# Two decode layers on one core: an added idle product ahead of the second layer's second queries, and w2's second and third pieces cut elsewhere

## The chip, the cores and the metric

One core of a Trainium2 chip runs the program. The metric is the device time of one execution in microseconds, the median of several runs. TensorE is PE in the profile, VectorE DVE, ScalarE ACT, GpSimd POOL; SyncE's queue, which issues nearly all transfers, is SP.

## The reference, cut to what matters

One token goes through four steps: attention, MLP, attention, MLP. Both attentions use the same weights and caches, and so do both MLPs.

```python
def _A_ref(x, k_cache, v_cache, wq, wo):            # 32 heads, 4096 keys, 128 a head, D = 512
    q = (x @ wq).reshape(B, Sq, H, Dh).transpose(0, 2, 1, 3)
    p = softmax(einsum("bhqd,bhkd->bhqk", q, k_cache) * (Dh ** -0.5))
    return einsum("bhqk,bhkd->bhqd", p, v_cache)... @ wo
def _B_ref(x, w1, b1, w2, b2):                      # F = 1376
    return gelu(x @ w1 + b1) @ w2 + b2
x = x + A(layernorm(x)); x = x + B(layernorm(x))
x = x + A(layernorm(x)); x = x + B(layernorm(x))
```

Everything is float32. The k and v caches are 64 MB each (eight groups of 8 MB), so that the caches, read twice but for what is kept on the chip, make nearly all of the traffic.

## The kernel before, in words

The 32 heads are worked in eight groups of four heads (G = 8). For a group, the 4096 keys are cut into eight blocks c of 512. `scores` (L201) makes four products a block, one a head, into the PSUM tile pS; `exponentials` (L206) takes the row maximum on DVE and the exponential on ACT (L214); `weights` (L217) turns the exponentials with four TensorE transposes into pO and copies them out on DVE (L222); `values` (L232) makes four products a block with the v cache into pO; `head` and `out_product` (L256, L276) normalize and multiply by wo. The queries of the next group are made by `query_block` (L189), sixteen small products into pO, and `queries` (L194), which turns pO on DVE (L150).

Nearly all of SBUF is one tile, `arena`, cut by hand: a ring of three homes of 8 MB (A_AT, B_AT, C_AT) for whole groups of k or v, and behind them places for weights (SHARED, SCRATCH, PAIR) that w1, w2, wo, wq and pieces of k use one after the other. All loads go out on SP's queue through `load` (L78), in program order. A load whose place is still being read, or was written by an earlier load, waits on SP for that; every load behind it waits as well. Products keep their program order on TensorE (`matmul`, L83). The order of DVE's and ACT's instructions is the program builder's: it may put a later line ahead of an earlier one. What waits for what follows from which bytes of the arena or of PSUM two instructions share.

**The change of layers.** The first layer ends with group 7. Its k lies in C_AT, its v in A_AT, and most of group 6's v is kept in B_AT, the rest in six PSUM banks pK. The second layer begins with group 7's k and v, which are still there, and goes on with group 6's v. In between stands the first MLP (`mlp`, L285). It multiplies x by four rows of w1 at SHARED; after row c's products it issues piece c of w2 into the same place, as W2_AT_CHANGE (L49) cuts it, and a fifth piece behind the first DVE step (L302). A piece is a range of w2's eleven blocks of 256 KB. Then come gelu and the eleven blocks of the second product (L310), eight passes on TensorE each. Behind blocks 3, 7 and 9, `behind_w2` (L435) issues the load of wq for the second layer's second queries (1 MB, SHARED, where blocks 0 to 3 lay) and the first six quarter blocks of group 6's k. Behind blocks 4, 7 and 10 stands `idle` (L165): a product with a zero operand and as streaming operand the first 512 or 256 columns at C_AT, whose result nothing uses.

**The second layer's start** (L450 to L485). First queries, then eight blocks of scores against group 7's k in C_AT. When block 0 is scored, `begin_k` (L430) loads four quarter blocks of group 6's k over it, at C_AT (L458); when block 1 is scored, four more; behind block 5 the rest (L460), then a pair of weights (L462). Then come `exponentials`, the second queries' `query_block` (L464), which reads wq at SHARED, `queries`, `weights`, and `values` against A_AT. ACT copies group 6's v out of the PSUM banks (L476): the first two copies go to SHARED and SHARED + U, where wq's first two blocks lie, once these are read. When A_AT's last block is used, SP issues group 5's k into it (8 MB). Scores and values of group 6 follow, and from there five more groups in the ring.

Of the kernel before, what the change touches and what calls it, by code (L numbers as in the profile page):

```python
# [25 lines left out]
FB = 11  # L26
W1C = FJ * J
EPS = 1e-5
U = 512
# [16 lines left out]
BY_PE = 3  # L46
W1_AT_END = ((0, 2), (2, 3), (3, 4))
LAST = ((0, 4), (4, 6), (6, 7), (7, 8))
W2_AT_CHANGE = ((0, 2), (2, 5), (5, 8), (8, 10), (10, 11))  # L49
W2_AT_END = ((0, 4), (4, 8), (8, 10), (10, 11))  # L50


# [1 line left out]
def decode_layers(ctx: ExitStack, tc: tile.TileContext, x, k, v, w, w1, b1, w2, b2, out):  # L54
# [10 lines left out]
    def small(name, n=1):  # L65
        if name not in places:
            a = sum(b - a for a, b in places.values())
            places[name] = a, a + n
        a, b = places[name]
        assert b <= 160 and b - a == n  # L70
        return smalls[:, a:b]
# [3 lines left out]
    def at(first, n):  # L75
        return arena[:, first : first + n]

    def load(first, src):  # L78
        t = at(first, src.shape[-1])
        tc.keep_in_program_order(nc.sync.dma_start(t, src))  # L80
        return t

    def matmul(*a, **kw):  # L83
        tc.keep_in_program_order(nc.tensor.matmul(*a, **kw))  # L84
# [7 lines left out]
    def of_w(row, i, n):  # L92
        return w[row][:, NC * i : NC * (i + n)]
# [24 lines left out]
    pS, pO = (psum.tile([P, 512], F32, name=n) for n in ("pS", "pO"))  # L118
# [9 lines left out]
    def of_32(t, n, i=0):  # L128
        return t[:, : 32 * n].rearrange("p (c q) -> p c q", q=32)[:, :, i]
# [9 lines left out]
    def pairs(t):  # L139
        return t[:, :8].rearrange("p (c i) -> p c i", i=2)  # L140

    def turned(src, wide=False):

        t = work.tile([P, P], F32, name="turned")
        if wide:
            for j in range(J):
                q = slice(32 * j, 32 * j + 32)
                nc.vector.transpose(t[q], src[q, P * j : P * (j + 1)])  # L148
        else:
            nc.vector.transpose(t, src[:, :P])  # L150
        return t

    def set_x(xin0, scale, xin1, queries=True):
        s = small("x_sum")
        t = x_wide if queries else small("x1", 8)
        if not queries:
            nc.gpsimd.memset(pairs(t)[:, :, 1], 1.0)
        x = pairs(t)[:, :, 0]
        nc.vector.scalar_tensor_tensor(x, xin0, scale, xin1, op0=ALU.mult, op1=ALU.add, accum_out=s)
        if queries:  # L160
            for j in range(1, J):
                nc.gpsimd.tensor_copy(pairs(t[:, 32 * j :])[:, :, 0], x)  # L162
        return t, s

    def idle(to, n=U):  # L165
        matmul(to[:, :n], zero[:, 0:1].to_broadcast([P, P]), at(C_AT, n), start=True, stop=True)
# [6 lines left out]
    def mean_of(xs, s):  # L173
        nm = minus_mean(s, pS[:, 0:1])
        xc, sq, ss, negm = small("xc", 4), small("sq", 4), small("ss"), small("negm")
        nc.vector.tensor_scalar(xc, pairs(xs)[:, :, 0], nm, None, op0=ALU.add)
        nc.vector.scalar_tensor_tensor(sq, xc, 1.0, xc, op0=ALU.mult, op1=ALU.mult, accum_out=ss)
        nc.vector.tensor_copy(negm, nm)
        return negm, ss

    def rstd_of(ss):
        nv = minus_mean(ss, pS[:, 1:2])
        ve, r = small("ve"), small("rstd")
        nc.vector.tensor_scalar(ve, nv, -1.0, EPS, op0=ALU.mult, op1=ALU.add)
        nc.vector.memset(pS[:, 0:2], 0.0)
        nc.gpsimd.tensor_tensor(r, ve, power, op=ALU.pow)
        return r

    def query_block(c, xs, wt):  # L189
        for j in range(J):  # L190
            matmul(pO[32 * j : 32 * j + 2, :P], pairs(xs)[:, c, :], wt[:, c, P * j : P * (j + 1)],
                   start=(c == 0), stop=(c == 3))
# [13 lines left out]
    def exponentials(sc, nsc):  # L206
        nc.vector.tensor_reduce(ml[:, 0:1], pS, axis=AX.X, op=ALU.max)  # L207
        mt, m, bias = work.tile([P, 32], F32, name="mt"), small("m"), work.tile([P, 32], F32, name="mt")
        nc.vector.transpose(mt, ml)
        nc.vector.tensor_reduce(m, mt[:, :C], axis=AX.X, op=ALU.max)  # L210
        nc.vector.tensor_scalar(mb[:, :C], m.to_broadcast([P, C]), nsc, None, op0=ALU.mult)
        nc.vector.transpose(bias, mb)  # L212
        p = at(SCRATCH, U)
        nc.scalar.activation(p, pS, AF.Exp, bias=bias[:, 0:1], scale=sc, accum_out=ml[:, 0:1])  # L214
        return p
# [69 lines left out]
    def mlp(xs, s, w1_t, w2_t, load_w2=None, behind_w2=None):  # L285
        xb = small("xb", 4)
        nc.gpsimd.tensor_tensor(xb, pairs(xs)[:, :, 0], b2c, op=ALU.add)
        for c in range(4):
            for j in range(J):
                matmul(pO[32 * j : 32 * j + 2, :FJ], pairs(xs)[:, c, :], w1_t[c][:, FJ * j : FJ * (j + 1)],  # L290
                       start=(c == 0), stop=(c == 3))
            if c == 0:
                nm, ss = mean_of(xs, s)
            if c == 1:
                r = rstd_of(ss)
            if load_w2:
                load_w2(c)
        idle(pS)
        ht = at(SCRATCH, 32 * FB)
        nc.vector.transpose(ht, pO[:, : 32 * FB])  # L300
        h, u, a, z, t, g = (small(f"gelu_{i}", FB) for i in "huaztg")
        nc.vector.scalar_tensor_tensor(h, of_32(ht, FB, 1), nm, of_32(ht, FB), op0=ALU.mult, op1=ALU.add)  # L302
        if load_w2:
            load_w2(4)
        nc.vector.scalar_tensor_tensor(u, h, r, b1c, op0=ALU.mult, op1=ALU.add)
        nc.vector.scalar_tensor_tensor(a, u, 0.044715, u, op0=ALU.mult, op1=ALU.mult)
        nc.vector.scalar_tensor_tensor(z, a, 1.0, u, op0=ALU.add, op1=ALU.mult)
        nc.scalar.activation(t, z, AF.Tanh, scale=float(np.sqrt(2.0 / np.pi)))
        nc.vector.scalar_tensor_tensor(g, t, 1.0, u, op0=ALU.add, op1=ALU.mult)  # L309
        for c in range(FB):  # L310
            for j in range(J):
                matmul(pS[32 * j : 32 * j + 1, :P], g[:, c : c + 1], w2_t[c][:, P * j : P * (j + 1)],
                       start=(c == 0), stop=(c == FB - 1))
            if load_w2:
                behind_w2(c)
                if c in (4, 7, FB - 1):
                    idle(pO, U if c == 4 else U // 2)
        return of_32(turned(pS), 4), xb

    def load_w1(first, a, b):  # L320
# [2 lines left out]
    def load_w2(first, a, b):  # L323
        load(first + U * a, w2[:, U * a : U * b])

    def in_rows(first, n, rows):
        return [at(first + n * i, n) for i in range(rows)]
# [107 lines left out]
    def behind_w2(c):  # L435
        if c == 3:
            load(SHARED, of_w((G - 1) % 2, G - 2, 1))
        if c == 7:
            begin_k(SHARED + NC, 4)
        if c == 9:  # L440
            begin_k(SHARED + 2 * NC, 2)

    own, xb = mlp(x1, s1, in_rows(SHARED, W1C, 4), in_rows(SHARED, U, FB),
                  lambda i: load_w2(SHARED, *W2_AT_CHANGE[i]), behind_w2)
    xs, s = set_x(own, 0.5, xb)
# [15 lines left out]
            k_t.append(at(KEPT_K, U))  # L461
    pair = load(C_AT + 24 * U, of_w(g % 2, g - 1, 2))  # L462
    p = exponentials(sc, nsc)
    for c in range(4):  # L464
        query_block(c, xs, wq_t)
    z = queries(pO, negm)
# [20 lines left out]
    for n in range(2, G):  # L487
# [18 lines left out]
        own = head_out(rl, wo_t, last=True)  # L506
    x1, s1 = set_x(own, 1.0, acc, queries=False)
    own, xb = mlp(x1, s1, in_rows(A_AT, W1C, 4), in_rows(A_AT + 11 * U, U, FB))
    y = small("y", 4)
    nc.vector.scalar_tensor_tensor(y, own, 0.5, xb, op0=ALU.mult, op1=ALU.add)  # L510
# [43 lines left out]
```

## Time and profile before

| | |
|---|---|
| median of 3 runs | 673.06 us (672.82 to 673.77) |
| the profiled execution's own time | 673.26 us |
| its span | 671.5 us |
| moved into SBUF | 285.88 MB, 426 GB/s over the span |
| PE / DVE / ACT / POOL busy | 59% / 49% / 3% / 1% of the span |

The profiled execution took 0.20 us more than the median. The span runs from the first to the last instruction; 1.8 us of the execution lie around it. A transfer's time to landing counts from its issue on SP, so that issue plus time is the moment it has landed. A product in float32 is two passes in the profile, so a count of products there is twice that of the code.

### The profile page before, as it was taken

The numbers are of one execution on the slowest core, as the hardware profiler recorded it, in microseconds if no ns is written. First come the engines' busy times: TensorE is split into PE (matmuls) and PEld (weight loads), VectorE is DVE, ScalarE is ACT, GpSimd is POOL, SyncE is SP. The second block draws the span as 40 slices with busy tenths as digits, with TensorE's granted clock in tenths as the row PEclk, the third lists the DMA queues.
The fourth block names the chain that finished last, engine by engine and source line by source line (L and its number), as shares of the span: only waits on it lengthen the run. The fifth ranks groups of instructions, "written<-read, shape, count | busy, mean of one in ns | idle before, by whom it ended". The sixth has DMA issues, their size and how long they took to land. (4 is left out here: it accounts for less than half of the span.)

```text
span 671.5 us, 5755 instructions
## 1 busy us (share of the span) xinstructions
PE 397.1 (59%) x2458; PEld 107.2 (16%) x2458; DVE 330.9 (49%) x483; ACT 22.5 (3%) x48; POOL 4.4 (1%) x21
## 2 busy tenths in 40 slices
PE   4443753647618456386877878747527466275585
PEld 1100110111202111011213222211102111021122
DVE  2049276393682845930112221294682945927631
ACT  0010000000000000001000110000000000000000
POOL 1000000000000000000000000000000000000000
PEclk9666775976868767677978898978668857687698
DMA  9999999999999999999999999999999999999997
GB/s 375 437 438 434 437 434 437 402 466 437 437 434 401 430 439 437 437 438 423 429 412 403 431 427 432 418 451 438 434 437 409 459 433 427 433 437 413 431 421 299
DMA packets 11545, 286.25 MB, mean 426 GB/s; under 512 B 1792, under 2 KB 1792, under 8 KB 3584
## 3 DMA queue, kind: packets, MB, share of 16 engines
q1 hardware_dynamic: 11088, 285.88, 99.1%
q8 instruction: 19, 0.31, 0.2%
q10 hardware_dynamic: 432, 0.01, 0.0%
q14 instruction: 6, 0.05, 0.0%
HBM read 285.88 MB, written 0.00 MB: 426 GB/s over the span
## 5 line engine op out<-in xcount | busy, mean ns | idle before, releaser
L84 PE MATMUL pS<-arena,zq 128*8 128x512 f32 x1024 | 137.3, 697 | 35.2 <-DMA arena<-in_k 31.4
L243 DVE TENSOR_TENSOR arena<-arena,turned 128x10240 f32<-128x10240 f32 x11 | 119.1, 10826 | 41.8 <-DMA arena<-in_v 41.8
L84 PE MATMUL pO<-arena,turned 128*4 128x512 f32 x584 | 98.1, 832 | 53.5 <-DMA arena<-in_v 51.9
L84 PE MATMUL pO<-arena,smalls 128*4 128x512 f32 (+3 forms) x158 | 30.4, 813 | 133.3 <-DVE arena L248 128.0
L248 DVE TENSOR_TENSOR arena<-arena 128x2048 f32<-128x2048 f32 (+1 forms) x33 | 98.5, 2985 | 0.7
L207 DVE TENSOR_REDUCE ml<-pS 128x1 f32<-128x512 f32 x16 | 11.1, 692 | 152.1 <-PE pS L84 152.1
L84 PEld LDWEIGHTS pS<-arena,zq 128*8 128x8 f32 x1024 | 29.3, 100 | 149.6 <-issue 112.7
L84 PE MATMUL pO<-arena,on_wide 128*128 128x512 f32 (+1 forms) x136 | 49.2, 527 | 4.0 <-DVE on_wide L266 2.7
L84 PE MATMUL pS<-arena,x_wide 128*128 128x512 f32 x88 | 41.0, 608 | 2.4 <-DMA arena<-in_w 2.4
L258 DVE STREAM_TRANSPOSE arena<-pO 128x512 f32<-128x512 f32 x16 | 11.5, 717 | 58.2 <-PE pO L84 58.2
L84 PEld LDWEIGHTS pO<-arena,turned 128*4 128x4 f32 x584 | 16.6, 104 | 119.2 <-issue 115.3
L214 ACT ACTIVATE arena<-pS,mt,smalls 128x512 f32<-128x512 f32 x16 | 12.4, 777 | 493.3 <-DVE mt L212 493.3
L219 PE MATMUL pO<-ident,arena 128*128 128x128 f32 x64 | 10.6, 291 | 30.5 <-DVE turned L148 16.4
L148 DVE STREAM_TRANSPOSE turned<-pO 32x128 f32<-32x128 f32 x64 | 19.8, 309 | 17.8 <-PE pO L84 17.1
L84 PEld LDWEIGHTS pO<-arena,smalls 128*4 128x4 f32 (+2 forms) x158 | 3.1, 88 | 145.1 <-DVE arena L248 137.1
L84 PEld LDWEIGHTS pO<-arena,on_wide 128*128 128x128 f32 (+1 forms) x136 | 19.4, 164 | 34.9 <-issue 28.1
L84 PE MATMUL pO<-arena,x_wide 128*2 128x128 f32 (+1 forms) x88 | 16.2, 396 | 9.6 <-POOL x_wide L162 6.7
L84 PEld LDWEIGHTS pS<-arena,x_wide 128*128 128x128 f32 x88 | 16.1, 193 | 32.6 <-DMA arena<-in_w 16.9
L84 PE MATMUL pS<-arena,smalls 128*1 128x128 f32 (+1 forms) x188 | 14.3, 316 | 2.3 <-DVE smalls L309 1.2
L148 DVE STREAM_TRANSPOSE turned<-pS 32x128 f32<-32x128 f32 x44 | 13.7, 311 | 0.8
L219 PEld LDWEIGHTS pO<-ident,arena 128*128 128x128 f32 x64 | 7.0, 145 | 43.2 <-issue 25.1
L224 DVE STREAM_TRANSPOSE mt<-ml 128x32 f32<-128x32 f32 x16 | 3.4, 212 | 17.0 <-ACT arena L214 17.0
(73 smaller groups left out, 95.6 us busy)
## 6 DMA issues: line engine op xcount, KB each, us to landing
arena<-in_w SPq DMA_DIRECT2D x13, 2048.0 KB, 11.5
arena<-in_k SPq DMA_DIRECT2D x4, 4096.0 KB, 25.3
arena<-in_v SPq DMA_DIRECT2D x2, 4096.0 KB, 39.1
arena<-in_w SPq DMA_DIRECT2D x6, 1024.0 KB, 20.4
arena<-in_v SPq DMA_DIRECT2D x3, 2048.0 KB, 43.3
arena<-in_v SPq DMA_DIRECT2D x1, 6144.0 KB, 29.6
arena<-in_w SPq DMA_DIRECT2D x6, 688.0 KB, 30.6
arena<-in_v SPq DMA_DIRECT2D x4, 1024.0 KB, 46.4
```

The lines of the kernel that those rows point to most:

```text
L84: tc.keep_in_program_order(nc.tensor.matmul(*a, **kw))
L148: nc.vector.transpose(t[q], src[q, P * j : P * (j + 1)])
L207: nc.vector.tensor_reduce(ml[:, 0:1], pS, axis=AX.X, op=ALU.max)
L214: nc.scalar.activation(p, pS, AF.Exp, bias=bias[:, 0:1], scale=sc, accum_out=ml[:, 0:1])
L219: tc.keep_in_program_order(nc.tensor.transpose(pT[:, b].rearrange("p j r -> p (j r)"), p[:, P * b : P * (b + 1)], ident))
L224: nc.vector.transpose(lt, ml)
L243: nc.vector.tensor_tensor(t, t, w.unsqueeze(2).to_broadcast([P, 4 * J * (C - BY_PE), P]), op=ALU.mult)
L248: nc.vector.tensor_tensor(a, a, b, op=ALU.add)
L258: nc.vector.transpose(ot, pO)
```

## The change

The second piece of w2 ends one block earlier, so that the third begins one block earlier; the wide idle product of the MLP moves from behind block 4 to behind block 3; and an idle product of 512 columns into pO is put ahead of the second queries' products in the second layer.

```diff
-W2_AT_CHANGE = ((0, 2), (2, 5), (5, 8), (8, 10), (10, 11))
+W2_AT_CHANGE = ((0, 2), (2, 4), (4, 8), (8, 10), (10, 11))
...
             if load_w2:
                 behind_w2(c)
-                if c in (4, 7, FB - 1):
-                    idle(pO, U if c == 4 else U // 2)
+                if c in (3, 7, FB - 1):
+                    idle(pO, U if c == 3 else U // 2)
...
     pair = load(C_AT + 24 * U, of_w(g % 2, g - 1, 2))
     p = exponentials(sc, nsc)
+    idle(pO)
     for c in range(4):
         query_block(c, xs, wq_t)
     z = queries(pO, negm)
```

## Rows read from the trace of the kernel before

**Rows 1.** The page: the span, and the load queue (packets, MB, share of 16 engines).
```profile
span 671.5 us, 5755 instructions
...
q1 hardware_dynamic: 11088, 285.88, 99.1%
```

**Rows 2.** The timeline of SP: start us, us, engine, line, operation, one load each.
```profile
357.47 0.33 SPq L80 DMA_DIRECT2D arena<-in_w  x1
...
359.15 0.33 SPq L80 DMA_DIRECT2D arena<-in_w  x1
...
361.76 0.33 SPq L80 DMA_DIRECT2D arena<-in_w  x1
...
364.55 0.33 SPq L80 DMA_DIRECT2D arena<-in_w  x1
...
371.64 0.33 SPq L80 DMA_DIRECT2D arena<-in_k  x1
...
377.65 0.33 SPq L80 DMA_DIRECT2D arena<-in_w  x1
...
390.02 0.33 SPq L80 DMA_DIRECT2D arena<-in_k  x1
```

**Rows 3.** DMA issues, the same seven loads: KB, us to landing (last: 8192 KB).
```profile
arena<-in_w SPq DMA_DIRECT2D x1, 768.0 KB, 5.6
...
arena<-in_w SPq DMA_DIRECT2D x1, 768.0 KB, 5.8
...
arena<-in_w SPq DMA_DIRECT2D x1, 256.0 KB, 5.1
...
arena<-in_w SPq DMA_DIRECT2D x1, 1024.0 KB, 5.8
...
arena<-in_k SPq DMA_DIRECT2D x1, 1024.0 KB, 7.8
...
arena<-in_w SPq DMA_DIRECT2D x1, 2048.0 KB, 17.2
...
arena<-in_k SPq DMA_DIRECT2D x1, 24.3
```

**Rows 4.** The timeline of PE in the MLP's second product: blocks 0-4, idle, 5-7.
```profile
362.93 1.77 PE L84 MATMUL pS<-arena,smalls 128*1 128x128 f32 x40
...
364.63 1.12 PE L84 MATMUL pO<-arena,smalls 128*128 128x512 f32 x2
...
365.69 0.84 PE L84 MATMUL pS<-arena,smalls 128*1 128x128 f32 x24
```

**Rows 5.** The timeline of PE: last scores, second queries, transposes, values of group 7.
```profile
376.55 1.04 PE L84 MATMUL pS<-arena,zq 128*8 128x512 f32 x8
...
377.41 1.06 PE L84 MATMUL pO<-arena,x_wide 128*2 128x128 f32 x32
...
380.33 0.66 PE L219 MATMUL pO<-ident,arena 128*128 128x128 f32 x4 [1.86 <-ACT arena L214]
...
381.40 8.55 PE L84 MATMUL pO<-arena,turned 128*4 128x512 f32 x64 [0.42 <-DVE turned L222]
```

**Rows 6.** The timeline of ACT and of DVE in the same stretch.
```profile
377.92 1.07 ACT L476 COPY arena<-pK 128x512 f32<-128x512 f32 x2 [15.25 <-PE pO L84]
...
379.40 0.78 ACT L214 ACTIVATE arena<-pS,mt,smalls 128x512 f32<-128x512 f32 x1 [0.41 <-DVE mt L212]
...
378.97 0.31 DVE L150 STREAM_TRANSPOSE turned<-pO 128x128 f32<-128x128 f32 x1
...
379.20 0.17 DVE L212 STREAM_TRANSPOSE mt<-mb 128x32 f32<-128x32 f32 x1
```

**Rows 7.** Windows: us; PE, PEld, DVE, ACT, POOL busy; granted clock; DMA share; GB/s.
```profile
377.70:381.10 3.40, 1.42 (x33) 0.87 (x24) 2.42 (x12) 1.94 (x4) 0.00 (x0) 0.99 1.11 470
381.10:384.50 3.40, 3.10 (x16) 0.56 (x20) 0.32 (x3) 0.00 (x0) 0.00 (x0) 0.50 1.04 449
384.50:387.90 3.40, 3.40 (x36) 0.78 (x32) 0.00 (x0) 0.00 (x0) 0.00 (x0) 1.00 0.92 390
```

## The prediction, made before the changed kernel ran

> **What bounds the kernel.** The page comes first: the load queue's packets take 99.1% of sixteen engines' span [rows 1]. A kernel like this gets faster only if the queue runs dry less often, and slower only if it runs dry more often; shorter work on TensorE is worth nothing by itself. So the question at each edit is whether a load goes out in time.
>
> To answer it, set the timeline of SP (when a load goes out) beside the DMA issues (how long until it lands) [rows 2, 3]. Two figures come out. The first is the queue's rate when it is full: the pair of weights issued at 377.65 lands at 394.85, the 8 MB behind it at 390.02 + 24.3 = 414.32, so 8.39 MB took 19.47 us, 431 GB/s. The second is what a late load costs. I call **slack** the time between a load's issue and the landing of the load ahead of it. The wq load goes out at 364.55; the last piece of w2, ahead of it, lands at 361.76 + 5.1 = 366.86: slack 2.31. It lands at 370.35, 3.49 us behind that piece, where 1.05 MB at 431 GB/s take 2.43. So 1.06 us were lost there. Piece 3 of w2 had a slack of 3.92 (issue 359.15, piece 2's landing 357.47 + 5.6 = 363.07) and landed 1.88 us later, where 0.79 MB take 1.82: next to nothing lost. If loss grows one for one below some slack, that slack is 2.31 + 1.06 = 3.37. This is an estimate from these rows, and I use it below: **a load is free of loss while its slack stays above 3.4 us.**
>
> **The change part by part.**
>
> *w2's pieces.* The same five loads carry the same bytes. Piece 2 is 256 KB smaller and so lands 0.6 us earlier (0.26 MB at 431 GB/s), at about 362.5; piece 3 is larger by as much and ends at the same byte, so it still lands near 364.95. Both are still released by the same rows of w1: blocks 2 and 3 lie over rows 0 and 1, blocks 4 to 7 over rows 1 and 2. Piece 3's slack shrinks to 362.5 − 359.15 = 3.3, at the edge: a loss of 0 to 0.1 us. Even that would not reach the end: the wq load behind it is late by its own issue, not by the queue, and would take up the 0.1 in its 1.06. What sets that issue is block 3's products. Blocks 0 to 4 run from 362.93 without a pause for 1.77 us [rows 4]; the smaller piece 2 only moves blocks 2 and 3's data from 363.07 to 362.5, and TensorE reaches them later than either. So 364.55 stays. From below, a gain is excluded by this; from above, 0.1 us. I take 0.
>
> *The idle product behind block 3.* Block 4 now runs behind the idle product rather than ahead of it, and waits for the larger piece. Before, the idle product and what follows it start 1.06 us apart (364.63 to 365.69), and 24 passes take 0.84 [rows 4]. Eight passes go from one side to the other. Piece 3 has landed (364.95) before the idle product is done, so TensorE waits no longer. The sum of passes up to block 7 is the same; the k load behind block 7 moves by 0.3 us at most if piece 3 holds block 4 up. Its slack is 370.35 − 366.6 or so, 3.7, and 0.3 less leaves it at the edge again. I take 0, and 0 to 0.3 for the range.
>
> *The idle product ahead of the second queries.* It brings two passes of 512 columns, but also a **wait** that the diff does not show: it streams the first 512 columns at C_AT, and the load of four quarter blocks of k over them went out at 371.64 and lands at 371.64 + 7.8 = 379.44 [rows 2, 3]. The last scores are done near 377.5 [rows 5]. So TensorE, whose products keep their order, stands for some 2 us. Then 1.06 for the idle product [rows 4] leaves the second queries at 380.5 instead of 377.41, done at 381.6 [rows 5]. Behind them: DVE turns pO (0.31 [rows 6]), and the transposes of the exponentials, which write pO, can start near 381.95 instead of 380.33. Values follow 1.07 behind the transposes as before, at 383.0: 1.6 us late.
>
> Now the clock. Values took 8.55 us [rows 5]; from 381.40 to 384.50 the granted clock was 0.50, the 1.2 GHz level, after a stretch in which TensorE was busy for 1.42 of 3.40 us at 0.99; from 384.50 it was 1.00, the 2.4 GHz level [rows 7]. At 2.4 GHz throughout they would need 8.55 − 3.1/2 = 7.0. The new stretch up to 381.1 holds about 1.6 us of work (379.5 to 381.1), little more than before, so I let the clock be low up to 384.50 again: 1.5 us at half rate do 0.75 of the 7.0, and values end at 384.5 + 6.25 = 390.75 instead of 389.95. If the idle product keeps the clock up, they end at 390.0. If it stays low for a stretch more, up to 387.9: 4.9 us do 2.45, the end is 392.45.
>
> What hangs on this end is one load: 8 MB of group 5's k into A_AT, issued at 390.02 with a slack of 394.85 − 390.02 = 4.83 us. 0.8 us later it still has 4.0, above 3.4: **no loss**. With the clock up the delay is nothing; at the late bound (2.5) the slack is 2.3 and about 1.0 us is lost. No load of SP stands behind the idle product before that one (the pair of 377.65 waits for scores alone). Were the 8 MB in the queue ahead of it not there, the whole delay would count.
>
> The loads after it are safer still: the next waits for scores that come 9 us later, with 8 MB queued ahead.
>
> *Sum:* 0 + 0 + 0 against the profiled execution's 673.26, which stands 0.20 above the median; against the median, **673.1 us**, with 0 to 1.0 on top from the bounds, and a gain of at most what the 8 MB lost against the best rate, which is tenths.
>
> **The rivals.**
>
> *Slower: the exponentials wait behind two copies.* On ACT's queue the two copies of kept v (L476) ran at 377.92, ahead of the exponential (L214) at 379.40 [rows 6], though they stand behind it in the program. They overwrite wq's first blocks, so they wait for the second queries, 0.51 us after these start. If the builder keeps that order, the idle product's wait for k holds up the exponential too: copies at 381.0 to 382.1, exponential at once behind, transposes 0.93 later at 383.05, values at 384.1. TensorE then has little to do from 381.6 to 384.1, so the clock is likely low up to 387.9: 3.8 us do 1.9, the end is 393.0, 3.1 us late. The slack falls to 1.7, below the 3.4, and 1.65 us are lost: **674.7 us**. With the clock up the end is 391.1, and nothing is lost. For it: the order before. Against it: if the builder reckons with the k load's wait, it puts the exponential first, as the program has it. This decides once the values end more than 1.4 us late.
>
> The price rests on the one late load in the trace. The Trainium skill (DMA: Bandwidth & Descriptors, Specifications) gives a first-byte latency of about 0.6 us for loads issued by the sync engine; by that a slack of 1.7 would be ample and this rival would cost nothing. The wq load, with 2.31 us of slack, lost 1.06 [rows 2, 3], so the trace does not agree, and the row is what I use.
>
> *Faster: the clock.* If the idle product did not have to wait, and the clock stayed at 2.4 GHz, values would end at 381.4 + 7.0 = 388.4, and group 5's k would go out 1.6 us earlier. But that load lost next to nothing: against it stands a queue with 4.83 us in it. A few tenths at most, **672.7 us**. The landing at 379.44 speaks against even that.
>
> *The edit of w2 moves the wq load.* If TensorE did wait for piece 2 where I see none, or reached block 3's end sooner, the loss of 1.06 would change by the same amount. At best a few tenths.
>
> **How the numbers follow.** No change 0.60; the exponentials behind the copies 0.28, of which about two thirds with the low clock and its 674.7 and the rest at no loss; tenths faster 0.12. A measurement of this kernel can tell 0.2%, 1.35 us, from no change: 671.7 and 674.4 are the bounds. The second case lies at the upper one. So faster 0.05, within 0.2% 0.77, slower 0.18. The range reaches from 672.3 (a gain of tenths and a lower run) to 674.7.
>
> **What would show it.** In the trace after: the idle product ahead of the second queries is released by a DMA of k near 379.4; the values of group 7 end between 390 and 391; group 5's k goes out near there and lands near 414.3; the wq load still goes out near 364.55 and lands near 370.35. If the copies on ACT run before the exponential, and that load goes out at 393, the first rival holds. I would be wrong if group 5's k lands more than 1 us later or earlier against the start of the span while its issue is above the 3.4 us, or if the wq load's landing moves.

## The result, and the profile after

The changed kernel took 676.61 us in the median of 14 runs (674.19 to 678.08), the kernel before 673.77 in 14 runs beside them (672.82 to 674.77). The ratio is **1.0039 (95% interval 1.0025 to 1.0052)**: some 2.6 us slower. The forecast was no change, 673.1, with a range of 672.3 to 674.7. The profiled execution of the changed kernel took 676.84, with a span of 675.0.

The timeline of SP in the changed kernel, the seven loads that answer to [rows 2]:

```profile
357.53 0.33 SPq L80 DMA_DIRECT2D arena<-in_w  x1
...
359.23 0.33 SPq L80 DMA_DIRECT2D arena<-in_w  x1
...
362.29 0.33 SPq L80 DMA_DIRECT2D arena<-in_w  x1
...
364.64 0.33 SPq L80 DMA_DIRECT2D arena<-in_w  x1
...
371.92 0.33 SPq L80 DMA_DIRECT2D arena<-in_k  x1
...
377.93 0.33 SPq L80 DMA_DIRECT2D arena<-in_w  x1
...
392.91 0.33 SPq L80 DMA_DIRECT2D arena<-in_k  x1
```

And the DMA issues of the same seven loads, with KB and us to landing, which answer to [rows 3]:

```profile
arena<-in_w SPq DMA_DIRECT2D x1, 512.0 KB, 5.0
...
arena<-in_w SPq DMA_DIRECT2D x1, 1024.0 KB, 6.5
...
arena<-in_w SPq DMA_DIRECT2D x1, 256.0 KB, 5.4
...
arena<-in_w SPq DMA_DIRECT2D x1, 1024.0 KB, 7.0
...
arena<-in_k SPq DMA_DIRECT2D x1, 1024.0 KB, 8.5
...
arena<-in_w SPq DMA_DIRECT2D x1, 2048.0 KB, 17.8
...
arena<-in_k SPq DMA_DIRECT2D x1, 24.5
```

Read them line by line, issue plus time. Piece 2 of w2 lands at 362.53, as foretold. Piece 3 goes out with a slack of 362.53 − 359.23 = 3.30 and lands at 365.73: 3.20 us behind piece 2 where 1.05 MB need 2.43, so 0.77 lost. The wq load lands at 371.64 instead of 370.35. The last line is the large one. Group 5's k goes out at 392.91 instead of 390.02. The pair ahead of it lands at 395.73, so its slack is 2.82 instead of 4.83, and it lands at 417.41 instead of 414.32: 21.68 us behind the pair where 8.39 MB need 19.47, **2.2 us lost**.

Why it goes out so late stands in the timeline of PE, which answers to [rows 5] (the first line is the end of the scores, of which the first passes lie ahead):

```profile
376.40 1.47 PE L84 MATMUL pS<-arena,zq 128*8 128x512 f32 x12
...
380.51 1.95 PE L84 MATMUL pO<-arena,smalls 128*128 128x512 f32 x2 [2.64 <-DMA arena<-in_k]
...
382.39 1.86 PE L84 MATMUL pO<-arena,x_wide 128*2 128x128 f32 x32
...
384.79 0.63 PE L219 MATMUL pO<-ident,arena 128*128 128x128 f32 x4 [0.54 <-DVE turned L150]
...
385.80 7.05 PE L84 MATMUL pO<-arena,turned 128*4 128x512 f32 x64 [0.38 <-DVE turned L222]
```

TensorE stood for 2.64 us until the k load over C_AT had landed (371.92 + 8.5 = 380.42). Then the added idle product took 1.88 us up to the next product, and the second queries 1.86, where a product of this size in the MLP and the same queries took 1.06 each in the kernel before. The windows show the clock that they got; the columns are those of [rows 7]:

```profile
377.94:380.50 2.56, 0.00 (x0) 0.00 (x0) 1.50 (x5) 0.83 (x2) 0.00 (x0) 1.00 1.00 422
380.50:384.30 3.80, 3.74 (x34) 1.36 (x34) 0.93 (x5) 1.11 (x3) 0.00 (x0) 0.55 1.12 482
384.50:387.90 3.40, 2.72 (x24) 0.95 (x28) 0.67 (x3) 0.00 (x0) 0.00 (x0) 1.00 0.96 415
```

In the first line TensorE does nothing; in the second it works at a granted clock of 0.55, mostly the 1.2 GHz level, through the idle product and the queries; in the third it is at 2.4 GHz, so that the values ran in 7.05 us instead of 8.55. The fast values gave back 1.5 us, and the end is still 2.89 late.

ACT did not do what the first rival feared; its timeline, which answers to [rows 6]:

```profile
379.67 0.78 ACT L214 ACTIVATE arena<-pS,mt,smalls 128x512 f32<-128x512 f32 x1 [16.46 <-DVE mt L212]
...
383.11 1.07 ACT L477 COPY arena<-pK 128x512 f32<-128x512 f32 x2 [2.57 <-issue]
```

The exponential now runs ahead of the two copies. It was done at 380.5 and waited there for TensorE.

Two theories come out of this. **W**: the wait of the idle product for k, with the low clock behind it, makes group 5's k late. **P**: the smaller second piece makes piece 3 and the loads behind it late. Single profiles cannot divide the cost between them. The pair, for one, lands anywhere from 394.78 to 396.60 in the profiles with the old pieces. The ratios of five rounds of runs can.

### The profile page after: what moved, and what is told of

It reads as the page before. It is cut to its first block, busy times and chain, and to the rows that moved or that the text cites. A ratio compares the mean times of both kernels' runs of the same rounds, so it can differ in the third digit from the quotient of the medians.

```text
span 675.0 us, 5762 instructions
## 1 busy us (share of the span) xinstructions
PE 394.0 (58%) x2460; PEld 106.3 (16%) x2460; DVE 331.4 (49%) x483; ACT 22.5 (3%) x48; POOL 4.4 (1%) x21
## 4 chain that ended last, share of the span: by engine, by line
DMA 67%; PE 27%; DVE 4%; SPq 1%; issue 1%; another core or an unknown queue 0%; ACT 0%; POOL 0%; DVEq 0%; ACTq 0%
DMA arena<-in_k 47%; PE pS L84 15%; DMA arena<-in_v 12%; PE pO L84 11%; DMA arena<-in_w 8%; DVE arena L243 2%; DVE arena L248 1%; SPq L80 1%; DMA xcol<-in_x 1%; DVE turned L148 0%; PE pO L219 0%; DVE arena L258 0%; ACT arena L214 0%; DVE ml L207 0%
## 5 line engine op out<-in xcount | busy, mean ns | idle before, releaser
L84 PE MATMUL pS<-arena,zq 128*8 128x512 f32 x1024 | 135.9, 691 | 34.3 <-DMA arena<-in_k 30.5
L84 PE MATMUL pO<-arena,turned 128*4 128x512 f32 x584 | 94.9, 808 | 56.4 <-DMA arena<-in_v 54.8
```

## The experiments

Each ratio is to the kernel before on the same chip.

**The pieces alone.**

```diff
     p = exponentials(sc, nsc)
-    idle(pO)
     for c in range(4):
```

> w2's pieces and the MLP's idle product as in the changed kernel, no idle product ahead of the second queries. Theory W (the added idle product waits for the load of k over C_AT, near 380.4, runs at the low clock with the queries behind it, and sends group 5's k out 2.9 us late, when its queue is nearly dry): the large part is gone; what remains is what piece 3 (landing 365.73 instead of 364.95) and the wq load (371.64 instead of 370.35) lost, 0 to 0.9 us over the kernel before, and group 5's k goes out near 390. Rival P (the pieces are the cause: the queue runs dry ahead of the 1 MB piece, and the loss stays to the end): most of the 2.8 us remains, piece 3 lands near 365.7 again. Rival N (landing times there differ from run to run whatever the kernel): piece 3 and wq land as in the kernel before.

Measured: 1.0014 (1.0004 to 1.0024), 0.9 us slower. Piece 3 went out with a slack of 2.72, landed at 366.18 and lost 1.15; the wq load landed at 372.25. Group 5's k went out at 391.08 with a slack of 5.04 and lost nothing. So a smaller part of the cost is the pieces', and the larger one went with the idle product. Rival N holds in part: with the old pieces, too, the wq load lands anywhere from 370.3 to 372.1, so that its landing in one profile says little about the pieces.

**The idle product alone.**

```diff
     p = exponentials(sc, nsc)
+    idle(pO)
     for c in range(4):
```

> The kernel before with the idle product ahead of the second queries and nothing else. Theory W: TensorE stands until k has landed over C_AT (379.4), idle product and queries then take some 3.8 us at 1.2 GHz, group 5's k goes out near 392, 2 us late, and lands 1 to 2.2 us late: 1.5 to 2.5 us slower than the kernel before. Rival P: no more than 0.5 us slower.

Measured: 1.0027 (1.0010 to 1.0044), 1.8 us slower. With the pieces' 0.14% this makes 0.41%; the whole change cost 0.39%. The timeline of PE in this kernel:

```profile
380.61 1.30 PE L84 MATMUL pO<-arena,smalls 128*128 128x512 f32 x2 [2.79 <-DMA arena<-in_k]
381.84 1.89 PE L84 MATMUL pO<-arena,x_wide 128*2 128x128 f32 x32
...
385.54 7.05 PE L84 MATMUL pO<-arena,turned 128*4 128x512 f32 x64 [0.38 <-DVE turned L222]
```

The same picture with the old pieces: 2.79 us of waiting for k, and the queries in 1.89 instead of 1.06. Group 5's k went out at 392.65, slack 3.63. In this one profile it lost only 0.2 us by its landing; this execution took 674.42, 0.9 less than this kernel's median.

**The same product without the wait.** The whole changed kernel, but the added idle product reads columns that nothing loads.

```diff
-    def idle(to, n=U):
-        matmul(..., at(C_AT, n), ...)
+    def idle(to, n=U, first=C_AT):
+        matmul(..., at(first, n), ...)
...
-    idle(pO)
+    idle(pO, first=A_AT)
     for c in range(4):
```

> The changed kernel whole, but the added idle product streams 512 columns of group 7's v at A_AT, which have lain there since the first layer, instead of those at C_AT: same product, no wait. Theory W: the product starts behind the last scores near 377.7, values end no later than 390, and group 5's k loses nothing: 0 to 0.9 us over the kernel before, as the kernel with the pieces alone. Rival T (the product's own work on TensorE's path is the cost): still 2 us or more slower.

Measured: 1.0008 (0.9998 to 1.0019). The timelines of PE and SP:

```profile
378.30 1.12 PE L84 MATMUL pO<-arena,smalls 128*128 128x512 f32 x2
379.36 1.06 PE L84 MATMUL pO<-arena,x_wide 128*2 128x128 f32 x32
...
382.35 7.05 PE L84 MATMUL pO<-arena,turned 128*4 128x512 f32 x64 [0.41 <-DVE turned L222]
...
389.46 0.33 SPq L80 DMA_DIRECT2D arena<-in_k  x1
```

The product took 1.06 us up to the next one, as a product at 2.4 GHz does, the values 7.05, and group 5's k went out at 389.46, earlier than in the kernel before. Its slack was 6.67. The product is not the cost; what it reads is. Nor did the earlier load gain anything.

**The same wait with a quarter of the product.**

```diff
     p = exponentials(sc, nsc)
+    idle(pO, P)
     for c in range(4):
```

> The kernel before with an added idle product of 128 columns at C_AT instead of 512: the same wait, a quarter of the product. Theory W, by wait alone: queries start near 379.6, values end at 390.5 to 391.9, by the clock that they get; group 5's k goes out 0.5 to 1.9 us late and loses 0 to 1.2 us, so 0 to 1.2 us slower, less than the kernel with the idle product of 512 columns alone by up to 1.2. Rival T: the loss falls to a quarter, 0.5 us or less, although k is waited for until 379.4. Rival P: nothing.

Measured: 1.0030 (1.0016 to 1.0045), as much as with the whole product, and above what I gave it. The timeline of PE:

```profile
381.48 0.59 PE L84 MATMUL pO<-arena,smalls 128*128 128x128 f32 x2 [3.24 <-DMA arena<-in_k]
382.00 1.89 PE L84 MATMUL pO<-arena,x_wide 128*2 128x128 f32 x32
```

The k load landed at 381.39, TensorE started behind it, the queries took 1.89, and group 5's k went out at 392.88. So a cost by the length of the product alone (0.5 us or less was given for that) is excluded, and the wait with the low clock behind it is enough for a cost as large. How much the length adds is not shown: the short product saved 0.7 us here (0.52 up to the queries instead of 1.23), but in this profile k also landed 0.8 later than in the one above (380.57), and the two intervals would hide as much.

**TensorE as late, the load not.** The whole changed kernel, with the late load in two halves.

```diff
         acc, pt, rl = group(z, acc, ahead, blocks(k, g, k_home,
-            HALVES if final else ((0, C),)))
+            HALVES if final or n == 2 else ((0, C),)))
         if not final:
```

> The changed kernel whole, with group 5's 8 MB of k in two loads of 4 MB, so that the first goes out when the values are half done. TensorE is as late as in the changed kernel. Theory W with the queue as the only way to the end: the first half goes out near 389.4 with a slack above 6 us and loses nothing, and the idle product's part of the cost (1.8 us) is gone: 0 to 1.2 us over the kernel before, the part of the pieces. Rival T (late work on TensorE costs by another way than this load): still 2 to 3 us slower.

Measured: 1.0013 (1.0002 to 1.0023), as the kernel with the pieces alone. SP's timeline and the DMA issues of the pair and the two halves:

```profile
378.16 0.33 SPq L80 DMA_DIRECT2D arena<-in_w  x1
...
388.96 0.33 SPq L80 DMA_DIRECT2D arena<-in_k  x1
...
392.39 0.33 SPq L80 DMA_DIRECT2D arena<-in_k  x1
```

```profile
arena<-in_w SPq DMA_DIRECT2D x1, 2048.0 KB, 17.9
...
arena<-in_k SPq DMA_DIRECT2D x1, 4096.0 KB, 16.8
...
arena<-in_k SPq DMA_DIRECT2D x1, 4096.0 KB, 23.0
```

The idle product still waited for k, and the values started at 385.28. But the first half went out at 388.96, with 7.1 us in the queue ahead of it; the two halves landed 9.70 and 9.63 us behind one another, where 4.19 MB take 9.73. Nothing was lost, and the idle product's whole part of the cost was gone.

**The load late by itself: three idle products, then six.** The kernel before, with `idle` as in the edit that reads A_AT: products in front of the values, behind everything that the added product delays.

```diff
     pt, rl = weights(p)
+    for _ in range(3):
+        idle(pS, first=A_AT)
     for c in range(C):
         values(c, pt, quarters(A_AT + NC * c), c)
```

> The kernel before with three idle products of 512 columns of v at A_AT, written into pS, between the transposes of the exponentials and the values: no wait on a load, nothing ahead of the queries, only group 5's k later. They end some 4.2 us after 381.4, values then take 7.0 at 2.4 GHz, so the load goes out near 392.7, 2.7 us late, slack 2.1 to 3.5. Theory W: the same cost as the idle product alone, 1 to 2.5 us slower. By the prediction's straight rule (loss only below 3.4, one for one): 0 to 1.3 us. Rival T2 (it was the wait's effect on other work ahead of the values, the queries or ACT's copies): no cost.

Measured: 0.9999 (0.9989 to 1.0009). It missed its dose: the three products took 2.67 us, not 4.2, and the values, at 2.4 GHz behind them, 7.05. Group 5's k went out at 390.93, 0.9 late, slack 5.66. That much costs nothing.

```diff
-    for _ in range(3):
+    for _ in range(6):
```

> The kernel before with six idle products between the transposes of the exponentials and the values, where three made group 5's k only 0.9 us late (slack 5.7, no cost). Each more costs 0.85 us at 2.4 GHz: the load goes out near 393.5, 3.5 us later than in the kernel before, slack 1.4 to 3.1. No idle product ahead of the queries, no wait for k there. Theory W (the late load is the whole of the idle product's cost): 1.5 to 3 us slower. Rival T2 (the wait costs through the queries or ACT's copies): no cost, as with three.

Measured: 1.0025 (1.0013 to 1.0036), 1.7 us slower. Its load of group 5's k:

```profile
393.25 0.33 SPq L80 DMA_DIRECT2D arena<-in_k  x1
```

```profile
arena<-in_k SPq DMA_DIRECT2D x1, 24.5
```

The pair ahead of it landed at 395.83, so the slack was 2.58. It landed at 417.75, 21.92 behind the pair: 2.45 us lost. No product waits for k here, the second queries run as before, and the cost is that of the idle product.

**Six idle products, and the load in halves.** The edit of the two-halves kernel on top.

```diff
-            HALVES if final else ((0, C),)))
+            HALVES if final or n == 2 else ((0, C),)))
         if not final:
```

> The same six idle products, and group 5's k in two loads of 4 MB, the first released when the values are half done, near 390, slack above 4.5. Theory W: the cost of the kernel with six idle products is gone or below 0.7 us, though TensorE is as late. Rival T: the cost stays.

Measured: 1.0007 (0.9999 to 1.0016). The first half went out at 389.75 with a slack of 6.11. Most of the cost is gone; the remainder is not told from none. In this profile a later load, 2 MB of v issued at 426.35, had a slack of 3.45 and lost 1.2 us, which may be the rest; this execution (676.04) was the slowest of this kernel's 12.

**The pieces without the moved idle product.**

```diff
-W2_AT_CHANGE = ((0, 2), (2, 5), (5, 8), (8, 10), (10, 11))
+W2_AT_CHANGE = ((0, 2), (2, 4), (4, 8), (8, 10), (10, 11))
```

> The kernel before with only the numbers of w2's pieces changed; the MLP's idle product stays behind block 4. If the smaller second piece is what costs (piece 3's slack falls from 3.9 to 3.3 us): piece 3 lands about 1 us later than in the kernel before, and the time is 0.3 to 1.5 us longer, as with the pieces and the moved idle product together (0.95). If the moved idle product is what costs: no change within 0.5 us.

Measured: 1.0024 (1.0011 to 1.0037), 1.6 us slower, just above the 1.5 that was given. The timeline of PE:

```profile
363.26 1.05 PE L84 MATMUL pS<-arena,smalls 128*1 128x128 f32 x32 [1.11 <-DVE smalls L309]
366.05 0.60 PE L84 MATMUL pS<-arena,smalls 128*1 128x128 f32 x8 [1.74 <-DMA arena<-in_w]
366.59 2.08 PE L84 MATMUL pO<-arena,smalls 128*128 128x512 f32 x2
368.59 1.15 PE L84 MATMUL pS<-arena,smalls 128*1 128x128 f32 x24
```

Block 4 waits 1.74 us for piece 3, landed at 366.00, and the idle product, which stood in that gap in the changed kernel, now comes behind it and takes 2.00 up to the next product, where it took 1.06 at 2.4 GHz. The k load behind block 7 goes out at 369.81 instead of 366.58. So the moved idle product is not what costs. That it hides a part of the pieces' cost is argued from this gap; the times do not show it, since the intervals of 1.0024 and of 1.0014 overlap.

**Piece 3 in two loads.**

```diff
-W2_AT_CHANGE = ((0, 2), (2, 4), (4, 8), (8, 10), (10, 11))
+W2_AT_CHANGE = (((0, 2),), ((2, 4),), ((4, 6), (6, 8)), ((8, 10),), ((10, 11),))
...
-                  lambda i: load_w2(SHARED, *W2_AT_CHANGE[i]), behind_w2)
+                  lambda i: [load_w2(SHARED, *ab) for ab in W2_AT_CHANGE[i]], behind_w2)
```

> The kernel with the changed pieces and the moved idle product, without the one ahead of the second queries, with piece 3 (1 MB, blocks 4 to 7) as two loads of 512 KB one behind the other, issued at the same place. Theory S (slack: piece 2 holds back 256 KB that row 1 of w1 had made room for, and the queue runs dry ahead of piece 3): its first half lands 0.7 to 1.2 us late against 1.23 us of transfer, the second loses nothing, and the time is that of the same kernel with one load, 0.5 to 1.4 us over the kernel before. Rival Z (one load of 1 MB with rows of 8 KB is itself slower than loads of 512 or 768 KB): the loss goes, 0 to 0.3 us over the kernel before.

Measured: 1.0002 (0.9992 to 1.0013). By the time the size of the one load is what costs; by the profile the first half was late all the same, landing 3.72 us behind piece 2 with a slack of 2.78. The two disagree, and the interval touches that of the pieces alone, so by the times it stays open whether the size of the load or its slack costs. A load of the old size speaks for slack: in the kernel with the little product, piece 3 of 768 KB happened to go out with a slack of 3.3 us and lost 0.8, as 1 MB did in the changed kernel.

**Both mended.** The idle product reads A_AT, and block 4 goes out with blocks 2 and 3, as early as in the kernel before.

```diff
-W2_AT_CHANGE = ((0, 2), (2, 4), (4, 8), (8, 10), (10, 11))
+W2_AT_CHANGE = (((0, 2),), ((2, 4), (4, 5)), ((5, 8),), ((8, 10),), ((10, 11),))
...
-    idle(pO)
+    idle(pO, first=A_AT)
```

> The changed kernel with both suspected costs taken out: the idle product ahead of the second queries streams v at A_AT, which needs no wait, and w2's blocks go out as early as in the kernel before, (0,2), then (2,4) and (4,5) one behind the other, then (5,8), with the MLP's idle product still behind block 3. Theory W with the pieces' part from bytes held back: both parts are gone, within 0.1% of the kernel before, piece (5,8) loses less than 0.3 us. If the pieces' part comes from the moved idle product: 0.1 to 0.15% slower remains. If the kernel gained from the two idle products themselves it would be faster by tenths of a us; the kernel with the delay alone speaks against that.

Measured: 0.9996 (0.9987 to 1.0005). Piece 3 landed at 365.04, 1.90 behind the load ahead of it, where 0.79 MB take 1.82. Both parts of the cost are gone. So is any gain: with the two idle products where the change wants them and no wait, group 5's k went out at 388.78 with 7.87 us in the queue, and the time is the kernel before's.

**The other way: two loads sent earlier.** The kernel before, with wq's load and group 5's k in halves.

```diff
-        if c == 3:
-            load(SHARED, of_w((G - 1) % 2, G - 2, 1))
+        if c in (1, 3):
+            h = U * (c - 1)
+            load(SHARED + h, of_w((G - 1) % 2, G - 2, 1)[:, h : h + NC // 2])
...
-            HALVES if final else ((0, C),)))
+            HALVES if final or n == 2 else ((0, C),)))
```

> The kernel before with two loads sent out earlier: wq's second-query block in two halves, the first behind block 1 of w2 (near 363.6 instead of 364.55), and group 5's k in two halves, the first when the values are half done. If the dry queue near 364 to 371 costs the kernel before 1 us or more, this gains 0.3 to 1.2 us. If the loss there only moves to the next load, or the cost of one more load is as large, no change within 0.5 us.

Measured: 1.0001 (0.9990 to 1.0013). The first half of wq went out at 364.05 instead of 364.55 and still lost 1.35 us. Half a microsecond earlier does not fill that gap. Group 5's k went out in halves here, the first at 385.01, and the time is still that of the kernel before: here nothing was gained by cutting a load that was not late.

## Why the prediction was wrong

**Right:** what bounds the kernel, and where to look. The wait for k at C_AT was read out of the diff and the issues; the load that hangs on it, group 5's k, is the one that carries the cost, as the kernels with that load in halves show. That fast work on TensorE gains nothing by itself was right too, twice (1.0008 and 0.9996, with group 5's k out 0.6 and 1.2 us earlier than before).

**The term that failed first: "Then 1.06 for the idle product", and 1.06 for the queries.** They took 1.88 and 1.86. The text held the clock low up to 384.50 and charged that only to the values, from 383.0 on; the idle product and the queries, at 379.4 to 381.6 in its reckoning, were priced from rows at 2.4 GHz. In the trace the low stretch (0.55 from 380.50 to 384.30) lay on these two, and the values ran at 2.4 GHz. The wait also ended 1.0 later (380.42, not 379.44); the landing of that load was taken from one profile, and with the old pieces it lies anywhere from 379.3 to 381.4. So the values started at 385.80, not 383.0, and ended near 392.85, not 390.75. The price of standing still was 2.64 us of wait and 1.6 us of slow work behind it.

**The term that failed second: "a load is free of loss while its slack stays above 3.4 us", losing one for one below.** It was drawn through one row. For group 5's k the profiles show, against 19.47 us of transfer, the first two columns below. The traces also keep the sixteen steps in which each load's completion is counted; its landing is the last of them. The other two columns count from the first step of the pair to the first step of group 5's k:

| kernel | slack, us | lost, us | lead on the first step, us | lost at the first step, us |
|---|---|---|---|---|
| before | 4.83 | 0.0 | 3.04 | 0.15 |
| three idle products | 5.66 | 0.4 | 2.69 | −0.14 |
| idle product alone | 3.63 | 0.2 | 0.72 | 1.16 |
| little idle product | 3.72 | 0.8 | 1.53 | 0.68 |
| changed | 2.82 | 2.2 | 0.98 | 0.91 |
| six idle products | 2.58 | 2.45 | 0.45 | 1.96 |

At 2.82 the rule gives 0.6, and the row says 2.2. Counted to the landings, the loss goes from tenths to more than two within a microsecond. Counted to the first steps, it grows one for one below a corner near 2 us, as the text supposed: in all runs nineteen loads went out with a lead of less than 1.5 us on the first step of the load before them (one of them 0.75 us behind it), and for each of them lead and loss add up to 1.7 to 2.4 us, while slack and loss to the landings add up to 2.3 to 5.2. With leads of 1.5 to 3 us most loads lost less than 0.5, some up to 1.2. So below the corner the form of the rule held; what failed is that it counted to the last of the sixteen steps. Had the delay alone been foretold right, the rule as it stood would still have given 673.7, inside no change. By first steps the same loads of the kernel before give another price, as an estimate: the wq load went out 1.08 us ahead and lost 0.96, a corner of 2.04; group 5's k has a lead of 3.04, of which a delay of 2.89 leaves 0.15, and 1.9 us are lost.

**The pieces: "a loss of 0 to 0.1 us", taken up by the wq load.** Piece 3 lost 0.77 at a slack of 3.30, and between 0.8 and 1.2 in the other profiles with one load of 1 MB there; with the old pieces it lost less than 0.1 in six of seven profiles. Whether the wq load behind it took that up cannot be read: it lost 1.5 in the changed kernel and 1.06 before, but anywhere from 1.0 to 2.9 in the profiles with the old pieces. In the time this part is 0.14% with the moved idle product.

**The rivals.** The builder put the exponential ahead of the copies, so the first rival's mechanism did not come. That its 393.0 and its 1.65 us of loss lie near what happened (392.91 and 2.2) is luck: the exponential was done at 380.5, and the delay came from the wait and the slow work ahead of the values.

**The Trainium skill** (DMA: Bandwidth & Descriptors, Specifications) gives about 0.6 us to a load's first byte. The trace disagrees here too: with six idle products the load went out 0.45 us ahead of the first step of the pair and lost 1.96 there, 2.4 us in all. The Trainium skill (DMA: Bandwidth & Descriptors, Why a DMA increments its semaphore by 16 and not by 1) also says that a load runs on up to 16 engines which finish independently. The traces agree: the sixteen steps of group 5's k lie 1.7 to 3.5 us apart, first to last, in the six kernels of the table. So a slack counted to the landing is too kind.

Of the changed kernel's loss, 0.91 us is there at the first step; up to the last it grows to 2.2, as the steps move from 1.84 us apart (the pair) to 3.18. With six idle products 1.96 is there at the first step already. Not shown: which engine makes which step, why the steps move apart, and how much of either part the whole time pays.

## What to carry to other kernels

An instruction that only keeps an engine warm must read something that nothing loads any more: with the operand under a transfer it stopped the engine for 2.64 us here, and the clock that it was meant to hold fell to 0.55 behind the stop. In a kernel bound by its load queue, price a delay by the load that hangs on it, and price the delay itself at the clock that the wait will leave. Do not take the slack that a load needs from one late load, and count it to the first step of the load ahead, not to its landing: here the corner lay near 2 us by the first step, and 2.8 us to the landing was too little. Let large loads go out in parts as their places come free: here that took away the whole cost of a late engine.

## What was not expected of the hardware

Two loads of 8 MB went out 2.82 and 2.58 us ahead of the last landing in the queue and still lost 2.2 and 2.45 us. The first step of the load ahead had come 1.84 and 2.14 us before that landing, so that on the first step they had a lead of only 0.98 and 0.45 us.

The clock of the values is not set by what stands in front of them alone. With the same products ahead of them they took 8.55 us in the kernel before, 8.75 in the one with the pieces alone and 7.05 in the one with two loads sent earlier. The lines of the last two:

```profile
382.27 8.75 PE L84 MATMUL pO<-arena,turned 128*4 128x512 f32 x64 [0.42 <-DVE turned L222]
...
381.33 7.05 PE L84 MATMUL pO<-arena,turned 128*4 128x512 f32 x64 [0.42 <-DVE turned L222]
```
